# Second batch of a fused attention and MoE kernel: softmax sums by products with ones, maxima joined by selection products, values ordered anew

## The chip, the cores and the metric

The kernel runs on one core of a Trainium2 chip. Its time is the device time of one launch in microseconds (us), as the median of several runs; lower is better. PE is the engine for matrix products, PEld its weight loads, DVE the vector engine, ACT the scalar engine with its table functions, POOL the general engine GpSimd, SP the engine that starts most DMA transfers. Products write to PSUM, everything else on the chip stands in SBUF.

## The reference

Eight batches of eight heads, 512 local and 32 global positions, head size 64. Local queries see the global keys and a window of 32 keys to each side; global queries see all keys. Both are softmaxed with a maximum subtracted and 1e-9 added to the sum. The result goes through a dense layer, a softplus and a second dense layer.

```python
s_g = scale * matmul(q_g, k_all.T);  out_g = matmul(sm(s_g), v_all)
s_ll = where(abs(pos[:, None] - pos[None, :]) <= 32, scale * matmul(q_l, k_l.T), -1e9)
s_l = concatenate([scale * matmul(q_l, k_g.T), s_ll], axis=-1)
out_l = matmul(sm(s_l), concatenate([v_g, v_l]))
x = concatenate([out_g, out_l], axis=2).transpose(0, 2, 1, 3).reshape(B * S, H * D)
h = x @ w_in;  g = maximum(h, 0) + log1p(exp(-abs(h)));  return g @ w_out
```

Here x has 4352 rows of 512, w_in is 512 x 2048 and w_out 2048 x 512. All inputs are float32; the two weights arrive as float64.

## The kernel before

**Dense layers.** The local rows of a batch (512 tokens) are one block, the 256 global rows of all batches one more at the end. For batch b and slice f of 16, a tile `h` of 128 x 512 is summed by twelve products (x and w each split into a high and a low part), in two halves of six; `act` makes the softplus from it (ACT `e`, DVE `e` L533, ACT `gh`, POOL `gl`), and four `opart` calls of three products add g times w_out to four tiles o0 to o3. The tiles `h` take turns in two PSUM slots (tag "h"); o0 to o3 have a bank each.

**Weights.** The float64 words are taken apart while batch 0 runs: per tile of 128 x 512 one ACT operation (L470), one one-input DVE operation (L477), two two-input ones (L479, L482), an ACT cast (L487) and a POOL subtract (L488). Their names are wbitswi, wiraw, wbitswo, woraw with the slice's number.

**Attention.** A pair m of heads is worked on at once; m = 0 to 3 are batch 0, which has code of its own (`turn0`, `split0`, and for the global queries `evict0g` with its tiles p0g1gh and p0g1gl, and `values0g` with o0g). Pairs from 4 on go through five pieces. `scores` (two halves p) writes keys by queries into a two-bank PSUM tile, to which for m < `MPE` = 8 the mask is added by a product; ACT copies it to s (L310), and DVE takes the maxima of 32 x 32 squares, turned (mt, L313). `maxima` has POOL copy three quadrants of mt to the first (L325), DVE reduces what belongs to a window (L328 to L332) and copies the result to all four quadrants (L338). `probs` spreads it by transposes (mb, L346), POOL subtracts (L355, L357) and ACT takes the exp (L358). `sums` does the same as `maxima` with sums of squares of the exps (zt, L368), adds 1e-9 (L371), inverts (L375) and spreads (rb, L377). `values` writes 32 PE instructions of values into v_ps, and DVE multiplies by rb into xa (L396). Scores, v_ps and the turned probabilities of batch 0 share one PSUM tile of two banks (tag "a"), so each waits until the one before was read.

**Order.** PE's order is that of the program. The dense items of batch 0 are written one after another, and between them the attention pieces whose due number is reached: pair m has its scores at 12m and 12m + 6 (with maxima and probs), its sums at 12m + 14, its values at 12m + 21. Every product has one line of the profile, L132, so PE's rows are told apart by tile names. The order of the other engines is made by a scheduler from the program.

Of the kernel before, what the change touches and what calls it, by code (L numbers as in the profile page):

```python
# [63 lines left out]
def moe_over_global_local_attention(  # L64
# [258 lines left out]
    def gather(mt, op):  # L323
        for a in range(1, 4):
            nc.gpsimd.tensor_copy(mt[0:32, GW * a:GW * a + GW], mt[32 * a:32 * a + 32, 0:GW])  # L325
        e0 = 4 * GW + 1
        for u, off in ((-1, 2), (2, 3)):
            nc.vector.tensor_reduce(grid(mt, e0 + u, (7, 6), (1, 2)), grid(mt, 4 + u - 2 * (u < 0), (12, 6), (1, 2), (off, 2), (GW, 4)), axis=AX.XY, op=op)  # L328
# [34 lines left out]

    def sums(m):
# [12 lines left out]
        nc.vector.transpose(rb.rearrange("p (s k) -> p s k", k=32), zr[:, 0:19].unsqueeze(2).to_broadcast([P, 19, 32]))  # L377
# [24 lines left out]
    def end(m):  # L402
        return 12 * m + 8 + LAG_V

    def pieces():
# [6 lines left out]
        for m in range(M0, M):  # L412
            for p in range(NPC):
# [3 lines left out]
                if p == 1:  # L417
                    fs.append(lambda m=m: maxima(m))
                    fs += [lambda m=m, q=q: probs(m, q) for q in range(NPC)]
                ps.append((12 * m + 6 * p, piece(*fs)))  # L420
            ps.append((12 * m + 8 + LAG_Z, lambda m=m: sums(m)))
# [323 lines left out]
```

## Time and profile before

| | us |
|---|---|
| median of 3 runs | 990.09 (990.07 to 990.39) |
| profiled execution | 991.48 |
| its span on the core | 989.7 |
| PE busy in it | 946.2 |
| DVE busy | 643.1 |
| ACT busy | 492.6 |
| POOL busy | 469.5 |

The profile is of one execution, and the runs' median is 1.39 below it. A row of a timeline has the start, the length, the engine, the line, the operation, the tiles (result, then inputs), the count, and in brackets the idle time before it with what ended it. Matmul rows of a group overlap, since the products are pipelined: how long a group occupies PE is the distance from its start to the next start. The table of slices on the page:

```profile
PE   6998598889999999999999999999999999999998
```

Each digit is a slice of 24.7 us, in tenths busy. Batch 0's own attention ends in the fourth slice, and pairs 4 to 7 stand in slices three to nine.

### The profile page before, as it was taken

To read this page: it belongs to the slowest core of one execution; us is meant where nothing else is said; L and a number is where in the kernel's file an instruction comes from. 1 tells how busy PE (TensorE), PEld (TensorE's weight loads), DVE (VectorE), ACT (ScalarE), POOL (GpSimd) and SP (SyncE) were. 2 spreads that over 40 slices of the span, in tenths; PEclk is the share of its full clock that TensorE was granted. 3 is DMA by queue.
4 is the path that set the end of the run, shared out by engine and by line. 5 is a ranking of instruction groups with operands and counts; after the bars stand their busy time and mean duration, and the time that the engine had idled before them with its cause. 6 is when DMAs were issued, how large, how long until landed. Compare 5 with 4: busy or idle time off the path is not lost.

```text
span 989.7 us, 14732 instructions
## 1 busy us (share of the span) xinstructions
PE 946.2 (96%) x5476; PEld 763.8 (77%) x5476; DVE 643.1 (65%) x1193; ACT 492.6 (50%) x811; POOL 469.5 (47%) x648
## 2 busy tenths in 40 slices
PE   6998598889999999999999999999999999999998
PEld 4776476668888788878887888878887888888896
DVE  5869898896667756786669666776668665411211
ACT  5756466544444544454445444454454445444453
POOL 4437776655445544444445544554445444322221
PEclk8998899999999999999999999999999999999999
DMA  9651331211112211121112111121112100100000
GB/s 357 231 188 46 122 111 57 65 66 41 47 47 69 69 47 46 48 74 47 47 37 72 47 47 47 66 71 47 47 33 88 32 17 1 65 1 1 10 35 22
DMA packets 30697, 64.60 MB, mean 65 GB/s; under 512 B 7328, under 2 KB 7840, under 8 KB 30624
## 3 DMA queue, kind: packets, MB, share of 16 engines
q1 hardware_dynamic: 29888, 63.32, 19.0%
q8 instruction: 43, 0.70, 0.3%
q10 hardware_dynamic: 736, 0.33, 0.2%
q14 instruction: 30, 0.25, 0.1%
HBM read 54.20 MB, written 9.44 MB: 64 GB/s over the span
## 4 chain that ended last, share of the span: by engine, by line
PE 67%; DVE 9%; POOL 4%; issue 3%; ACT 1%; DMA 1%; POOLq 0%; DVEq 0%; ACTq 0%
PE o L132 30%; PE h L132 29%; PE s_ps L132 5%; PE v_ps L132 4%; DVE xh L442 1%; DVE zt L368 1%; DVE xl L443 1%; POOL xl L443 1%; DVE mb L346 1%; POOL mt L325 1%; DVE s L312 1%; POOL s L355 1%; DVE xa L396 1%; DVE mt L332 0%; DVE e L533 0%
## 5 line engine op out<-in xcount | busy, mean ns | idle before, releaser
L132 PE MATMUL h<-xh,wi 128*128 128x512 f32 (+1 forms) x1152 | 341.9, 380 | 6.5 <-DVE e L533 5.8
L132 PE MATMUL o<-wo,gh 128*128 128x512 f32 x1088 | 344.8, 398 | 0.0
L537 POOL TENSOR_TENSOR gl<-e,gh 128x512 fp32r<-128x512 f32 x136 | 180.5, 1327 | 315.7 <-ACT gh L536 263.2
L132 PEld LDWEIGHTS h<-xh,wi 128*128 128x128 f32 x1152 | 211.1, 188 | 51.8 <-DVE e L533 8.9
L132 PEld LDWEIGHTS o<-wo,gh 128*128 128x128 f32 x1088 | 198.8, 188 | 46.0 <-issue 3.3
L533 DVE SCALAR_TENSOR_TENSOR e<-h,e 128x512 f32<-128x512 f32 x136 | 92.7, 682 | 210.1 <-ACT e L532 192.5
L132 PE MATMUL h<-xl,wi 128*128 128x512 f32 (+1 forms) x576 | 217.6, 378 | 0.9 <-DVE xl L443 0.9
L132 PE MATMUL o<-wo,gl 128*128 128x512 f32 x544 | 213.1, 392 | 0.2
L530 ACT ACTIVATE e<-h 128x512 f32<-128x512 f32 x136 | 81.0, 595 | 175.5 <-PE h L132 173.5
L536 ACT CAST gh<-e 128x512 fp32r<-128x512 f32 x136 | 84.5, 622 | 154.7 <-DVE e L533 154.5
L132 PEld LDWEIGHTS h<-xl,wi 128*128 128x128 f32 x576 | 108.4, 188 | 21.7 <-DVE xl L443 1.3
L355 POOL TENSOR_TENSOR s<-s,mb 128x640 f32<-128x640 f32 (+1 forms) x56 | 96.6, 1725 | 57.8 <-DVE mb L346 57.8
L132 PEld LDWEIGHTS o<-wo,gl 128*128 128x128 f32 x544 | 102.4, 188 | 23.2 <-POOL gl L537 1.1
L368 DVE TRANSPOSE_TENSOR_REDUCE zt<-s 128x32 f32<-128x1024 f32 x56 | 69.4, 1239 | 58.9 <-ACT s L358 58.7
L358 ACT ACTIVATE s<-s 128x1024 f32<-128x1024 f32 x56 | 59.4, 1061 | 83.5 <-POOL s L357 47.7
L532 ACT ACTIVATE e<-e,one 128x512 f32<-128x512 f32 x136 | 98.4, 723 | 4.3
L531 ACT ACTIVATE e<-e 128x512 f32<-128x512 f32 x136 | 85.9, 632 | 3.9
L313 DVE TRANSPOSE_TENSOR_REDUCE mt<-s 128x32 f32<-128x1024 f32 x56 | 68.9, 1231 | 3.7 <-ACT s L310 2.9
L132 PE MATMUL s_ps<-raw 64*128 64x192 f32 (+2 forms) x672 | 64.3, 325 | 0.6 <-issue 0.6
L132 PEld LDWEIGHTS v_ps<-s,v 128*64 128x64 f32 x896 | 49.4, 137 | 19.5 <-ACT s L310 6.5
L132 PE MATMUL v_ps<-s,v 128*64 128x96 f32 (+3 forms) x896 | 56.7, 280 | 7.3 <-ACT s L310 5.2
L132 PEld LDWEIGHTS s_ps<-raw 64*128 64x128 f32 x672 | 53.5, 192 | 11.6 <-issue 10.8
(147 smaller groups left out, 886.0 us busy)
## 6 DMA issues: line engine op xcount, KB each, us to landing
raw<-in_qk SPq DMA_DIRECT2D x32, 352.0 KB, 3.0
v<-in_v SPq DMA_DIRECT2D x28, 384.0 KB, 3.0
raw<-in_qk SPq DMA_DIRECT2D x28, 368.0 KB, 3.6
wiraw<-in_w_in SPq DMA_DIRECT2D x16, 512.0 KB, 8.5
woraw<-in_w_out SPq DMA_DIRECT2D x16, 512.0 KB, 7.4
out<-ot SPq DMA_DIRECT2D x32, 256.0 KB, 2.1
v<-in_v SPq DMA_DIRECT2D x4, 512.0 KB, 8.6
raw<-in_qk SPq DMA_DIRECT2D x4, 416.0 KB, 8.3
```

What stands on the lines that cost most here:

```text
L132: order["pe"] = after(nc.tensor.matmul(*a, **k), "pe").ins
L313: order["scores"] = nc.vector.tensor_reduce(windows(mt, 4 + 16 * p, 36, 2, 16), s.rearrange("p h (b k) -> p h b k", k=32), axis=AX.X, op=A ...
L355: nc.gpsimd.tensor_tensor(sw, sw, pairs(mb, 352, mo, md, w), op=ALU.subtract)
L358: nc.scalar.activation(s, s, AF.Exp, scale=0.125)
L368: nc.vector.tensor_reduce(windows(zt, 4 + 16 * p, 36, 2, 16), st["s", m, p].rearrange("p h (b k) -> p h b k", k=32), axis=AX.X, op=ALU.add ...
L443: (nc.vector if j % 2 else nc.gpsimd).tensor_tensor(lo, f(t), hi.bitcast(F32), op=ALU.subtract)
L530: nc.scalar.activation(e, ph, AF.Abs)
L531: nc.scalar.activation(e, e, AF.Exp, scale=-1.0)
L532: nc.scalar.activation(e, e, AF.Ln, bias=one)
L533: nc.vector.scalar_tensor_tensor(e, ph, 0.0, e, op0=ALU.max, op1=ALU.add)
L536: nc.scalar.copy(gh, e)
L537: nc.gpsimd.tensor_tensor(gl, e, gh.bitcast(F32), op=ALU.subtract)
```

## The change

For pairs 4 to 7 alone, three things are done in another way.

*Sums.* Instead of `sums`, `values` makes the sums itself: 16 products of the exps with a block of ones go to z_ps, a tile in an "h" slot, and to the free half of v_ps's second bank. There each sum stands on 64 rows. DVE then transposes 32 x 32 squares of both out of PSUM (z), adds 1e-9, joins the three parts of a global query's sum, inverts all 19 columns at once (zr) and spreads them (rb) as before.

*Maxima.* Four products with 0/1 matrices (`quads`) copy each quadrant of mt to all 128 rows of a PSUM tile m_ps (tag "a"). DVE's reductions read that and leave the result on all rows, so the POOL copies L325 and the DVE copies L338 are not needed. `quads` is filled by a POOL copy at the start.

*Order.* Maxima and probs of a pair are due at 12m + 8 (before: with the second scores at 12m + 6), values at 12m + 15 (before 12m + 21), where before them sums stood at 12m + 14. The tiles mb have three buffers instead of two. The start of batch 1's pieces (`first`) keeps its value. On SP's queue the v loads and the xg stores of these pairs come to stand ahead of some raw and weight loads.

```diff
+LAG_M = 2
+EARLY_V = 15
...
+    quads = const.tile([P, 4, P], F32, name="quads")
+    ones = const.tile([P, D], F32, name="ones")
+    nc.vector.memset(ones, 1.0)
+    one = ones[:, 0:1]
...
+        nc.gpsimd.tensor_copy(quads.rearrange("p a (c k) -> p a c k", c=4),
+                              identf.rearrange("p (a k) -> p a k", a=4).unsqueeze(2).to_broadcast([P, 4, 4, 32]))
...
-    def gather(mt, op):
-        for a in range(1, 4):
-            nc.gpsimd.tensor_copy(mt[0:32, GW * a:GW * a + GW], mt[32 * a:32 * a + 32, 0:GW])
+    def gather(mt, op, src=None):
+        rows = P if src is not None else 32
+        if src is None:
+            src = mt
+            for a in range(1, 4):
+                nc.gpsimd.tensor_copy(mt[0:32, GW * a:GW * a + GW], mt[32 * a:32 * a + 32, 0:GW])
         e0 = 4 * GW + 1
+        to = lambda start, *dims: grid(mt, start, *dims, rows=rows)
+        of = lambda start, *dims: grid(src, start, *dims, (GW, 4), rows=rows)
...
     def maxima(m):
-        e = gather(st.pop(("mt", m)), ALU.max)
+        mt = st.pop(("mt", m))
+        if m < MPE:
+            ps = ps_a.tile([P, 2, 512], F32, tag="a", name=f"m_ps{m}")[:, 0]
+            for a in range(4):
+                mm(ps[:, GW * a:GW * a + GW], lhsT=quads[:, a], rhs=mt[:, 0:GW], start=True, stop=True, skip_group_check=True)
+            st["e", m] = gather(mt, ALU.max, ps)
+            return
+        e = gather(mt, ALU.max)
...
-        mb = pl.tile([P, 2, 352], F32, tag="mb", name=f"mb{m}_{p}", bufs=2)
+        mb = pl.tile([P, 2, 352], F32, tag="mb", name=f"mb{m}_{p}", bufs=3)
...
+    def weighted(m, banks, lhs, seen):
+        for c, p, o, w, bank, at in VPARTS:
+            for h in range(2):
+                mm(banks[bank][64 * h:64 * h + 64, at:at + w], lhsT=lhs(h, c), rhs=st["s", m, p][:, h, o:o + w],
+                   start=(bank, h) not in seen, stop=(c, bank) in ((3, 0), (5, 1)), skip_group_check=True)
+                seen.add((bank, h))
+
+    def sums_pe(m, zs):
+        z = pl.tile([P, rows_of(608)], F32, tag="mb", name=f"z{m}", bufs=3)[:, 0:608]
+        for t, at, w in ((zs[0], 0, 384), (zs[1], 384, 224)):
+            nc.vector.transpose(z[:, at:at + w], t[:, 0:w])
+        zr = pl.tile([P, ROW], F32, tag="zr", name=f"zr{m}", bufs=2)
+        nc.vector.tensor_scalar(zr[:, 0:19].unsqueeze(2), windows(z, 0, 32, 19, 1), 1e-9, None, op0=ALU.add)
+        nc.vector.tensor_reduce(zr[:, 19:20], windows(z, 128, 224, 3, 1).rearrange("p a b -> p b a"), axis=AX.X, op=ALU.add)
+        nc.vector.tensor_scalar(windows(zr, 4, 7, 3, 1), zr[:, 19:20].unsqueeze(1).to_broadcast([P, 3, 1]), 1e-9, None, op0=ALU.add)
+        nc.vector.reciprocal(zr[:, 0:19], zr[:, 0:19])
+        spread(m, zr)
...
         ps = ps_a.tile([P, 2, 512], F32, tag="a", name=f"v_ps{m}")
-        parts = ((0, 0, 0, 160, 0, 0), (1, 0, 160, 192, 0, 64), (2, 0, 352, 160, 0, 192), (2, 1, 0, 32, 0, 352), (3, 1, 32, 96, 0, 288),
-                 (3, 1, 128, 96, 1, 0), (4, 1, 224, 192, 1, 32), (5, 1, 416, 96, 1, 128))
-        seen = set()
-        for c, p, o, w, bank, at in parts:
-            for h in range(2):
-                mm(ps[64 * h:64 * h + 64, bank, at:at + w], lhsT=vt[:, h, c], rhs=st["s", m, p][:, h, o:o + w],
-                   start=(bank, h) not in seen, stop=(c, bank) in ((3, 0), (5, 1)), skip_group_check=True)
-                seen.add((bank, h))
+        if m < MPE:
+            zs = (ps_h.tile([P, 512], F32, tag="h", name=f"z_ps{m}"), ps[:, 1, 256:512])
+            weighted(m, zs, lambda h, c: ones, set())
+        weighted(m, (ps[:, 0], ps[:, 1]), lambda h, c: vt[:, h, c], {(1, 0), (1, 1)} if m < MPE else set())
+        if m < MPE:
+            sums_pe(m, zs)
...
-        return 12 * m + 8 + LAG_V
+        return 12 * m + (EARLY_V if m < MPE else 8 + LAG_V)
...
+                tail = [lambda m=m: maxima(m)] + [lambda m=m, q=q: probs(m, q) for q in range(NPC)] if p else []
+                if m < MPE:
+                    if p:
+                        ps.append((12 * m + 6 + LAG_M, piece(*tail)))
+                    tail = []
+                ps.append((12 * m + 6 * p, piece(*fs, *tail)))
+            if m >= MPE:
+                ps.append((12 * m + 8 + LAG_Z, lambda m=m: sums(m)))
...
-    first = end(H // 2 - 1) + STEP
+    first = 12 * (H // 2 - 1) + 8 + LAG_V + STEP
```

Three places of the new order follow; the new file's lines are some 8 to 48 higher (L132 is L140).

PE around pair 4's values, before: h0_5 is the tile of slice 5, v_ps4 the values, o0_0 the first output tile.

```order
L132 MATMUL h0_5_1087<-xh0_3_627,wi5_613 128x512 x2
L132 MATMUL h0_5_1087<-xl0_3_628,wi5_613 128x512
L132 MATMUL v_ps4_1129<-s4_0_655,v4_145 64x160 x2
L132 MATMUL v_ps4_1129<-s4_0_655,v4_145 64x192 x2
L132 MATMUL v_ps4_1129<-s4_0_655,v4_145 64x160 x2
L132 MATMUL v_ps4_1129<-s4_1_703,v4_145 64x32 x2
L132 MATMUL v_ps4_1129<-s4_1_703,v4_145 64x96 x4
L132 MATMUL v_ps4_1129<-s4_1_703,v4_145 64x192 x2
L132 MATMUL v_ps4_1129<-s4_1_703,v4_145 64x96 x2
L132 MATMUL o0_0_889<-wo3_774,gh0_3_949 128x512 x2
```

After, the ones_73 products into z_ps4 and v_ps4 come first, then the values, and all of it stands in the middle of the output products of slice 1 (gh0_1, gl0_1).

```order
L140 MATMUL o0_1_894<-wo1_517,gl0_1_806 128x512
L140 MATMUL z_ps4_971<-s4_0_657,ones_73 64x160 x2
L140 MATMUL z_ps4_971<-s4_0_657,ones_73 64x192 x2
L140 MATMUL z_ps4_971<-s4_0_657,ones_73 64x160 x2
L140 MATMUL z_ps4_971<-s4_1_705,ones_73 64x32 x2
L140 MATMUL z_ps4_971<-s4_1_705,ones_73 64x96 x2
L140 MATMUL v_ps4_970<-s4_1_705,ones_73 64x96 x2
L140 MATMUL v_ps4_970<-s4_1_705,ones_73 64x192 x2
L140 MATMUL v_ps4_970<-s4_1_705,ones_73 64x96 x2
L140 MATMUL v_ps4_970<-s4_0_657,v4_146 64x160 x2
L140 MATMUL v_ps4_970<-s4_0_657,v4_146 64x192 x2
L140 MATMUL v_ps4_970<-s4_0_657,v4_146 64x160 x2
```

The group has moved ahead from between h0_5 and the outputs of slice 3 to between the first and last two outputs of slice 1.

DVE in the stretch in which mb4 (pair 4's spread maxima) is made and p0g1gl, the small copy for the last global output of batch 0, follows; before:

```order
L346 STREAM_TRANSPOSE mb4_1_724<-mt4_653 128x2x320
L479 SCALAR_TENSOR_TENSOR wbitswi8_877<-wiraw8_683,wbitswi8_877 128x512
L482 SCALAR_TENSOR_TENSOR wiraw8_683<-wiraw8_683,wbitswi8_877 128x512
L533 SCALAR_TENSOR_TENSOR e0_1_799<-h0_1_760,e0_1_799 128x512
L368 TENSOR_REDUCE zt4_963<-s4_0_655 128x2x16
L477 TENSOR_SCALAR wbitswo3_769<-wbitswo3_769 128x512
L255 COPY p0g1gl_815<-t0g1_808 32x128
L479 SCALAR_TENSOR_TENSOR wbitswo3_769<-woraw3_153,wbitswo3_769 128x512
```

After, from behind the second mb4:

```order
L524 SCALAR_TENSOR_TENSOR wbitswi8_878<-wiraw8_685,wbitswi8_878 128x512
L522 TENSOR_SCALAR wbitswo4_821<-wbitswo4_821 128x512
L527 SCALAR_TENSOR_TENSOR wiraw8_685<-wiraw8_685,wbitswi8_878 128x512
L524 SCALAR_TENSOR_TENSOR wbitswo4_821<-woraw4_681,wbitswo4_821 128x512
L575 SCALAR_TENSOR_TENSOR e0_1_800<-h0_1_740,e0_1_800 128x512
L522 TENSOR_SCALAR wbitswi10_1062<-wbitswi10_1062 128x512
L527 SCALAR_TENSOR_TENSOR woraw4_681<-woraw4_681,wbitswo4_821 128x512
L524 SCALAR_TENSOR_TENSOR wbitswi10_1062<-wiraw10_876,wbitswi10_1062 128x512
L522 TENSOR_SCALAR wbitswo5_838<-wbitswo5_838 128x512
L527 SCALAR_TENSOR_TENSOR wiraw10_876<-wiraw10_876,wbitswi10_1062 128x512
L524 SCALAR_TENSOR_TENSOR wbitswo5_838<-woraw5_683,wbitswo5_838 128x512
L263 COPY p0g1gl_816<-t0g1_809 32x128
```

The first sums of pair 4 (zt4) are gone; p0g1gl now stands behind ten weight operations and e0_1, where there were three, e0_1 and the reduction for zt4.

DVE where xa of pair 4 (xa1_0) is made, before: rb4 stood long ahead, and xa stands behind the maxima's transposes of pair 5.

```order
L346 STREAM_TRANSPOSE mb5_0_1064<-mt5_906 128x704
L346 STREAM_TRANSPOSE mb5_1_1069<-mt5_906 128x2x320
L479 SCALAR_TENSOR_TENSOR wbitswo8_1121<-woraw8_953,wbitswo8_1121 128x512
L533 SCALAR_TENSOR_TENSOR e0_5_1110<-h0_5_1087,e0_5_1110 128x512
L396 TENSOR_TENSOR xa1_0_1146<-v_ps4_1129,rb4_981 128x384
L396 TENSOR_TENSOR xa1_0_1146<-v_ps4_1129,rb4_981 128x224
L479 SCALAR_TENSOR_TENSOR wbitswo9_1175<-woraw9_1002,wbitswo9_1175 128x512
```

After, where z4 is the tile of the turned sums and zr4 its inverse:

```order
L415 STREAM_TRANSPOSE z4_1004<-v_ps4_970 128x224
L527 SCALAR_TENSOR_TENSOR wiraw11_929<-wiraw11_929,wbitswi11_1107 128x512
L417 TENSOR_SCALAR zr4_1007<-z4_1004 128x19
L418 TENSOR_REDUCE zr4_1007<-z4_1004 128x1
L419 TENSOR_SCALAR zr4_1007<-zr4_1007 128x3
L420 RECIPROCAL zr4_1007<-zr4_1007 128x19
L386 STREAM_TRANSPOSE rb4_1012<-zr4_1007 128x608
L438 TENSOR_TENSOR xa1_0_1014<-v_ps4_970,rb4_1012 128x384
L438 TENSOR_TENSOR xa1_0_1014<-v_ps4_970,rb4_1012 128x224
L575 SCALAR_TENSOR_TENSOR e0_4_1051<-h0_4_1028,e0_4_1051 128x512
```

xa now follows its own sums directly, ahead of e0_4, and the maxima of pair 5 come later.

More of the change, by code (lines that the diff above doesn't have):

```diff
@@ L315, in scores, with grid @@
         st["s", m, p] = s
-    def grid(t, start, *dims):
-        base = t[0:32, start:start + 1]
+    def grid(t, start, *dims, rows=32):
+        base = t[0:rows, start:start + 1]
         return bass.AP(base.tensor, base.offset, [list(base.ap[0])] + [list(d) for d in dims])
-    def gather(mt, op):
-        for a in range(1, 4):
-            nc.gpsimd.tensor_copy(mt[0:32, GW * a:GW * a + GW], mt[32 * a:32 * a + 32, 0:GW])
+    def gather(mt, op, src=None):
[4 more added lines that the diff above has]
+                nc.gpsimd.tensor_copy(mt[0:32, GW * a:GW * a + GW], mt[32 * a:32 * a + 32, 0:GW])
@@ L330, in gather @@
+        nc.vector.tensor_reduce(to(e0 + 1, (7, 6), (4, 2)), of(4 + 1, (12, 6), (7, 2)), axis=AX.X, op=op)
         g = e0 + 42
-        nc.vector.tensor_reduce(grid(mt, g, (1, 2)), grid(mt, 4 + 4, (36, 2), (12, 3), (3, 2), (GW, 4)), axis=AX.XYZ, op=op)
-        nc.vector.tensor_copy(grid(mt, e0 + 4, (21, 2), (7, 3)), mt[0:32, g:g + 2].unsqueeze(2).to_broadcast([32, 2, 3]))
+        nc.vector.tensor_reduce(to(g, (1, 2)), of(4 + 4, (36, 2), (12, 3), (3, 2)), axis=AX.XYZ, op=op)
+        order["maxima"] = nc.vector.tensor_copy(to(e0 + 4, (21, 2), (7, 3)), mt[0:rows, g:g + 2].unsqueeze(2).to_broadcast([rows, 2, 3])).ins
@@ L362, in moe_over_global_local_attention, with spread @@
     SEG = ((lambda t: t[:, 0:128].unsqueeze(1), 0, 1, 128), (lambda t: windows(t, 160, 224, 2, 192), 128, 2, 192))
+    def spread(m, zr):
+        rb = st["rb", m] = pl.tile([P, rows_of(608)], F32, tag="rb", name=f"rb{m}", bufs=1)[:, 0:608]
+        nc.vector.transpose(rb.rearrange("p (s k) -> p s k", k=32), zr[:, 0:19].unsqueeze(2).to_broadcast([P, 19, 32]))
     def sums(m):
@@ L375, in sums @@
             nc.vector.reciprocal(zr[32 * a:32 * a + 32, 0:19], z[0:32, 21 * h:21 * h + 19])
-        rb = st["rb", m] = pl.tile([P, rows_of(608)], F32, tag="rb", name=f"rb{m}", bufs=1)[:, 0:608]
-        nc.vector.transpose(rb.rearrange("p (s k) -> p s k", k=32), zr[:, 0:19].unsqueeze(2).to_broadcast([P, 19, 32]))
+        spread(m, zr)
+    VPARTS = ((0, 0, 0, 160, 0, 0), (1, 0, 160, 192, 0, 64), (2, 0, 352, 160, 0, 192), (2, 1, 0, 32, 0, 352), (3, 1, 32, 96, 0, 288),
+              (3, 1, 128, 96, 1, 0), (4, 1, 224, 192, 1, 32), (5, 1, 416, 96, 1, 128))
+    def weighted(m, banks, lhs, seen):
[13 more added lines that the diff above has]
+        nc.vector.reciprocal(zr[:, 0:19], zr[:, 0:19])
+        spread(m, zr)
     def values(m):
@@ L416, in pieces @@
                     fs.append(lambda m=m, p=p: load(m + 1, p))
[L417 to L421, printed above, removed]
+                tail = [lambda m=m: maxima(m)] + [lambda m=m, q=q: probs(m, q) for q in range(NPC)] if p else []
[6 more added lines that the diff above has]
+                ps.append((12 * m + 8 + LAG_Z, lambda m=m: sums(m)))
             fs = [lambda m=m: values(m)]
@@ L479, in bits_w @@
         note("dve", nc.vector.scalar_tensor_tensor(a, hi32, -0x80000000, a, op0=ALU.bitwise_and, op1=ALU.bitwise_or))
-        r = lo32 if k < NF - 1 else pl.tile([P, 512], I32, tag="mb", name=f"wlast{kind}", bufs=2)
+        r = lo32 if k < NF - 1 else pl.tile([P, 512], I32, tag="mb", name=f"wlast{kind}", bufs=3)
         note("dve", nc.vector.scalar_tensor_tensor(r, lo32, 29, a, op0=ALU.logical_shift_right, op1=ALU.bitwise_or))
@@ L497, in output_banks @@
         return banks["o"]
-    one = const.tile([P, 1], F32, name="one")
-    nc.vector.memset(one, 1.0)
     def moe_items():
```

5 lines of the change are left out of this document (2 added, 3 removed).

## The prediction

> **What bounds the kernel now.** I read the page first, its busy times and shares of the span of 989.7 us.
>
> ```profile
> PE 946.2 (96%) x5476; PEld 763.8 (77%) x5476; DVE 643.1 (65%) x1193; ACT 492.6 (50%) x811; POOL 469.5 (47%) x648
> ```
>
> TensorE (PE) is busy for 96% of the span, so whatever is added to PE costs its own length unless PE would have been idle there. The second view is the list of PE's waits, by what ended them (total us, times, longest).
>
> ```profile
> PE s_ps L132 <- DVE xa L396: 8.8, 2, 7.5
> PE h L132 <- DVE e L533: 5.8, 8, 1.7
> PE v_ps L132 <- ACT s L310: 5.2, 3, 3.4
> ...
> PE o0g L132 <- ACT p0g1gh L254: 2.7, 1, 2.7
> PE v_ps L132 <- DVE s L312: 2.1, 1, 2.1
> ...
> PE h L132 <- DVE xl L443: 0.9, 1, 0.9
> ```
>
> The third is a table of windows (length; busy time of PE, PEld, DVE, ACT, POOL with counts; granted PE clock; DMA share; GB/s).
>
> ```profile
> 120.37:124.11 3.74, 3.74 (x17) 2.49 (x18) 3.74 (x4) 1.57 (x3) 3.74 (x6) 0.54 0.00 0
> 77.41:83.52 6.11, 6.11 (x26) 4.83 (x26) 6.11 (x10) 5.65 (x11) 3.25 (x6) 0.66 0.13 50
> 217.00:989.00 772.00, 765.20 (x4350) 623.69 (x4348) 459.92 (x863) 368.80 (x565) 342.50 (x491) 1.00 0.14 45
> ```
>
> From 217 us on PE is busy for 765.20 of 772 us at a clock of 1.00, and the instructions there stay as they are: that stretch keeps its length. What the change can move lies before 217 us, and DVE is busy throughout both windows quoted from there. The timeline of PE around the stalls (start, length, what, count, idle time before and its releaser):
>
> ```profile
> 102.09 0.73 PE L132 MATMUL h<-xh,wi 128*128 128x512 f32 x2 [1.19 <-DVE e L533]
> ...
> 106.50 2.03 PE L132 MATMUL v_ps<-s,v 128*64 128x160 f32 x32 [1.40 <-ACT s L310]
> 108.46 0.73 PE L132 MATMUL o<-wo,gh 128*128 128x512 f32 x2
> ...
> 120.37 1.03 PE L132 MATMUL s_ps<-mask,ident 128*128 128x512 bf16 x2 [7.54 <-DVE xa L396]
> ```
>
> **What PE gains in work.** Four pairs (m = 4 to 7) each get 16 more products of the same shapes as the values products, with a block of ones in the place of v. A values group takes 108.46 - 106.50 = 1.96 us, so 4 x 1.96 = 7.8. Each also gets four selection products, 128 x 128 against 76 columns, two instructions apiece. The trace has none of that shape; the nearest is the turning of the probabilities, 128 columns:
>
> ```profile
> 70.32 1.39 PE L132 MATMUL t0g<-diag,e_g 128*128 128x128 f32 x10
> 71.64 0.74 PE L132 MATMUL h<-xh,wi 128*128 128x512 f32 x2
> ...
> 231.01 2.72 PE h L132 x12
> 233.74 1.36 PE o L132 x6
> ```
>
> Ten of them occupy 71.64 - 70.32 = 1.32, or 0.132 each; 4 x 8 x 0.132 = 4.2. The ends: no better than half that (76 of 128 columns are 0.6 of it, say 1.9 in all), no worse than a 512-column product (2.72 / 12 = 0.227, so 7.3). I take 4.2, the nearest row. Together **+12.0** (9.7 to 15.1).
>
> **What goes.** The waits on xa, on s (ACT and DVE), and on xl are 8.8 + 5.2 + 2.1 + 0.9 = 17.0, and the one of 1.19 at 102.09 lies in the same stretch: 18.2. They belong to places where values, xa and the scores behind them are ordered anew: values come earlier, sums no longer hang on POOL copies and two reductions of 1.2 us, so the old waits don't survive as such (which new ones appear is the next part). After the 7.54 wait PE ran at 0.54 of its clock for 3.74 us, which lost 3.74 x 0.46 = 1.7. A first pair of products after a wait shows 0.73, where others show 0.62: ten such places, 1.1. Together **-21.0**.
>
> A rule of the Trainium skill speaks to that clock: "TensorE: Matmul & The Clock Gate", in its section on HAM oscillation, has an idle window of about 3.4 us send the clock to half rate. The trace agrees for the wait of 7.54 (0.54 after it), but a wait of only 2.72 ahead of 77.41 also left 0.66, which the rule would not give. By the rule 1.7 would return and nothing else; the sum above takes the same 1.7.
>
> **What is new.** First the last global output, o0g1. Its second half needs p0g1gl, a small DVE copy.
>
> ```profile
> 72.29 1.55 DVE L479 SCALAR_TENSOR_TENSOR wbitswi<-wiraw,wbitswi 128x512 int32<-128x512 int32 x1
> 73.88 1.39 DVE L482 SCALAR_TENSOR_TENSOR wiraw<-wiraw,wbitswi 128x512 int32<-128x512 int32 x1
> 75.19 0.68 DVE L533 SCALAR_TENSOR_TENSOR e<-h,e 128x512 f32<-128x512 f32 x1
> ...
> 77.44 0.27 DVE L255 COPY p0g1gl<-t0g 32x128 f32<-32x128 f32 x1
> ...
> 80.46 0.68 DVE L479 SCALAR_TENSOR_TENSOR wbitswi<-wiraw,wbitswi 128x512 int32<-128x512 int32 x1
> ```
>
> Before, mb ends at 72.29 and the copy starts at 77.44. In the new order of DVE the copy stands behind seven two-input weight operations, three one-input ones and one e. The groups of this stretch give their means (busy us, mean ns):
>
> ```profile
> L482 DVE SCALAR_TENSOR_TENSOR woraw<-woraw,wbitswo 128x512 int32<-128x512 int32 x13 | 12.9, 1001 | 0.1
> ...
> L477 DVE TENSOR_SCALAR wbitswo<-wbitswo 128x512 int32<-128x512 int32 x13 | 9.4, 739 | 0.2 <-ACT wbitswo L470 0.2
> ...
> L377 DVE STREAM_TRANSPOSE rb<-zr 128x608 f32<-128x608 f32 x3 | 2.4, 800 | 0.0
> ```
>
> That is 7 x 1.00 + 3 x 0.74 + 0.68 = 9.9. mb itself ends 0.9 later than before: the selection products wait for half of h1 (1.36) and take 1.06, while copies of 1.56 (L338) go. So the copy ends at 72.29 + 0.9 + 9.9 + 0.27 = 83.4. The old gl products started 1.04 after 77.41, at 78.45; PE has 1.06 of selection products more ahead of them, which this wait swallows. New wait: 83.4 - 78.45 - 1.06 = **3.9** (0 if the operations take 0.68 and 0.43 each, 8 if each takes the 1.55 of the row at 72.29).
>
> Second, the chain from the sums to xa, at the place where the next scores want the same PSUM slot. For pair 4: two transposes out of PSUM (0.8 together, as the one of 608 columns), two weight triples that stand between (2 x (1.00 + 1.00 + 0.74) = 5.5 at the means, 2 x (0.68 + 0.68 + 0.43) = 3.6 unhindered), four small operations (0.9), the spread of the reciprocals (0.80) and two products to xa (0.9): 8.9, or 7.0 unhindered. PE covers it with the last six of the products with ones (0.7), v (1.96), o (1.36) and h (2.72): 6.7. That leaves 0.3 to 2.2 ahead of s5_1 and as much ahead of s6_1, which has the same cover; pairs 6 and 7 have another o or h and fewer weights between, so nothing. I take 0.6 for the first (PE is late there already by the wait above, while DVE works on) and 1.2 for the second: **1.8** (0 to 6, if operations double).
>
> Third, the products with ones need pair 5's exponentials, which now have from m5 to z5: four h halves and four o pairs of 1.36 each, and the scores of pair 6, two mask products at 0.227 and twelve of about 176 columns, 0.227 x 176 / 512 = 0.08 each: 10.9 + 1.4 = 12.3 us of PE work. The old kernel's row for pair 5 has its reductions at 113.17 and its last exp ending at 126.43:
>
> ```profile
> 113.17 0.53 DVE L328 TENSOR_REDUCE mt<-mt 32x12 f32<-32x96 f32 x2 [3.05 <-POOL mt L325]
> ...
> 125.37 1.06 ACT L358 ACTIVATE s<-s 128x1024 f32<-128x1024 f32 x1
> ```
>
> 13.26 against 12.3: **0.9** (0 to 3, as the queues fall). The new mask of quads on POOL pushes an early select back: 0.2. The DVE reductions that go (two of 1.2 us per pair), the three quadrant copies and POOL's gather copies free DVE time, but PE waits for DVE only where named, so they enter by the waits and not a second time. SP's order moves the xg stores and v loads of these pairs ahead of some raw and weight loads; in the windows above DMA is 0.13 or less busy, so nothing. New: 3.9 + 1.8 + 0.9 + 0.2 = **+6.8**.
>
> **The sum.** 12.0 + 6.8 - 21.0 = -2.2. The profiled execution took 991.48 us, 1.39 above the median of 990.09; it would take 989.3, and on the median's scale the forecast is 990.1 - 2.2 = **987.9**.
>
> **Rivals.** *The new waits don't come.* DVE has some 4 us less to do per pair and unhindered operations take 0.68; then the 6.8 fall away: 990.1 + 12.0 - 21.0 = 981.1. For it: 80.46 shows the short time right there, where POOL had nothing to do. Against it: DVE is busy all of both early windows. *DVE's two-input operations are held by POOL (slower).* The same operation took 1.55 at 72.29 and 0.68 at 80.46; at 72.29 POOL was in this:
>
> ```profile
> 71.72 1.58 POOL L355 TENSOR_TENSOR s<-s,mb 128x640 f32<-128x640 f32 x1 [1.78 <-DVE mb L346]
> ```
>
> The new order places the seven beside the same POOL subtracts, in one queue ahead of p0g1gl. If all 7 and the 8 of the two chains are held to 1.55 instead of their mean of 1.00, that is 15 x 0.55 = 8.3 more: -2.2 + 8.3 = +6.1, so 996.2. POOL was busy for 3.25 + 3.74 of the 9.85 us of the two early windows, 0.71: held for that share, their mean is 0.71 x 1.55 + 0.29 x 0.68 = 1.30, which adds 15 x 0.30 = 4.5 and gives 992.4. I price this rival midway, at 994.3. It turns the sign once their mean passes 1.00 + 2.2 / 15 = 1.15 us. The Trainium skill has this as a rule ("SBUF — State Buffer", section "Who interferes with whom"): a DVE operation with two SBUF inputs and GpSimd shut each other out for the whole instruction. The two rows agree; by it the slower rival is the outcome wherever POOL is busy. *The waits only change their names*: the products with ones wait for the exps and PE's added 12.0 fill what was idle, one for one; about 990. *The change doesn't act*: the new code covers only m < 8 and the rows of the order show it there; no chance of note.
>
> **How the numbers follow.** Forecast 0.44, first rival 0.22, slower rival 0.24, change of names 0.10. A measurement of this kernel can tell 0.2%, 2.0 us, from no change, so faster means under 988.1. The forecast lies at that edge: its 0.44 are 0.24 faster and 0.20 the same. Faster: 0.24 + 0.22 = 0.46. The same: 0.20 + 0.07 = 0.27. Slower: 0.24 + 0.03 = 0.27. The range of 8 in 10 takes in the first rival's time and the slower one's with a little of the selection products' upper end: 981.0 to 994.8. Above it lies the part of the slower rival in which everything is held, below it only a gain past the first rival. The bounds of the unknown shapes (9.7 to 15.1) alone give 985.6 to 991.0, inside it.
>
> **What would show it.** Right: a group of products with ones takes 1.96 and one of selection about 1.06; p0g1gl ends near 83 and o0g waits for it; the wait of 7.54 is gone; waits on xa of about 1 us ahead of s5_1 and s6_1; DVE's busy time falls by some 15 us; the stretch after the last pair of the second batch is as long as before. Wrong: any single new wait over 5 us, a clock under 0.9 in a window past 90 us, weight operations of DVE at a mean of 1.15 or more (slower rival) or 0.8 or less (first rival), or selection products at 0.23 each.

## The result and the profile after

The changed kernel took **1008.07 us** (median; 1005.39 to 1008.85) against 990.08 before: a ratio of 1.0177, 95% interval 1.0157 to 1.0196. The prediction was 987.9, its range 981.0 to 994.8; it was wrong by 20 us and in the sign.

The page of the profile after, and PE's waits (total us, times, longest):

```profile
span 1006.6 us, 14966 instructions
...
PE 961.3 (95%) x5629; PEld 779.7 (77%) x5636; DVE 632.1 (63%) x1157; ACT 493.4 (49%) x811; POOL 459.7 (46%) x621
```

```profile
PE z_ps L140 <- DVE e L575: 11.0, 2, 7.4
PE o0g L140 <- ACT p0g1gh L262: 5.7, 1, 5.7
...
PE h L140 <- DVE e L575: 4.0, 6, 1.1
PE s_ps L140 <- DVE xa L438: 3.3, 2, 3.0
...
PE o0g L140 <- DVE p0g1gl L263: 2.2, 1, 2.2
```

The waits of the old list on xa (8.8), s (7.3) and xl (0.9) are gone or small, as the prediction had it. But PE's idle time, span less busy, was 989.7 - 946.2 = 43.5 before and is 1006.6 - 961.3 = 45.3 now: other waits of the same sum stand in their place. The span grew by 16.9, of which idle time is 1.8 and PE's busy time 15.1. How much of the latter is new work shows in PE's timeline:

```profile
83.17 1.97 PE L140 MATMUL o0g<-p0g1gh,v 128*128 128x64 f32 x8 [5.66 <-ACT p0g1gh L262]
...
87.36 0.68 PE L140 MATMUL o0g<-p0g1gl,v 32*128 32x64 f32 x2 [2.23 <-DVE p0g1gl L263]
...
101.64 1.37 PE L140 MATMUL z_ps<-s,ones 128*64 128x160 f32 x20
102.84 0.82 PE L140 MATMUL v_ps<-s,ones 128*64 128x96 f32 x12
103.50 1.98 PE L140 MATMUL v_ps<-s,v 128*64 128x160 f32 x32
...
120.37 1.01 PE L140 MATMUL m_ps<-mt,quads 128*128 128x76 f32 x8
121.17 0.71 PE L140 MATMUL h<-xh,wi 128*128 128x512 f32 x2
...
141.52 2.51 PE L140 MATMUL z_ps<-s,ones 128*64 128x160 f32 x20 [7.43 <-DVE e L575]
```

At full clock the products with ones occupy 103.50 - 101.64 = 1.86 and the selection products 121.17 - 120.37 = 0.80: 4 x 2.66 = 10.6 for four pairs. The other 15.1 - 10.6 = 4.5 are put down to slow clock, by subtraction. The windows show where (length; busy PE, PEld, DVE, ACT, POOL; granted PE clock; DMA share; GB/s), after first, before second:

```profile
80.00:100.00 20.00, 14.25 (x57) 11.48 (x59) 13.10 (x18) 11.43 (x20) 11.53 (x10) 0.66 0.09 29
100.00:125.00 25.00, 21.66 (x150) 17.68 (x150) 15.46 (x29) 11.59 (x18) 7.43 (x7) 0.93 0.37 131
125.00:150.00 25.00, 17.42 (x119) 13.94 (x119) 22.25 (x23) 11.14 (x17) 17.34 (x14) 0.80 0.17 57
...
235.00:1006.00 771.00, 764.07 (x4345) 622.74 (x4343) 458.60 (x861) 367.07 (x563) 340.83 (x491) 1.00 0.14 45
```

```profile
80.00:100.00 20.00, 20.00 (x93) 15.10 (x93) 19.93 (x33) 11.15 (x20) 12.94 (x11) 0.84 0.11 32
100.00:125.00 25.00, 14.88 (x86) 10.88 (x86) 21.75 (x31) 12.32 (x20) 17.86 (x18) 0.86 0.29 107
```

Two things are to be seen. The last row of after is as long and as dense as the old one from 217 on, so all of the loss lies ahead of it. And DVE, which was busy for 41.7 of the 45 us from 80 to 125, is now busy for 28.6 there, and then for 22.25 of 25 from 125 to 150, where PE stands for 7.43 in one piece: its load has become uneven. That bunch, ahead of z5 at 141.52, in DVE's timeline:

```profile
122.18 1.09 DVE L522 TENSOR_SCALAR wbitswo<-wbitswo 128x512 int32<-128x512 int32 x3
123.18 1.63 DVE L366 STREAM_TRANSPOSE mb<-mt 128x704 f32<-128x704 f32 x2
124.74 2.98 DVE L524 SCALAR_TENSOR_TENSOR wbitswo<-woraw,wbitswo 128x512 int32<-128x512 int32 x2
127.64 2.05 DVE L522 TENSOR_SCALAR wbitswi<-wbitswi 128x512 int32<-128x512 int32 x1
...
137.65 1.52 DVE L524 SCALAR_TENSOR_TENSOR wbitswi<-wiraw,wbitswi 128x512 int32<-128x512 int32 x1
139.20 1.66 DVE L527 SCALAR_TENSOR_TENSOR wiraw<-wiraw,wbitswi 128x512 int32<-128x512 int32 x1
140.79 0.68 DVE L575 SCALAR_TENSOR_TENSOR e<-h,e 128x512 f32<-128x512 f32 x1
```

Five weight triples stand between pair 5's maxima and e0_6, the operation that frees the "h" slot for z_ps5. The exponentials are not what z5 waits for: ACT's last one ended at 134.19, when PE had just stopped. ACT is itself late by the same bunch. Its last two steps ahead of e0_6 (the later one at 138.23) stand in its order behind a weight's cast, and ahead of that cast it was idle for 1.93, until DVE had made the weight:

```profile
133.12 1.07 ACT L378 ACTIVATE s<-s 128x1024 f32<-128x1024 f32 x1
134.08 0.59 ACT L572 ACTIVATE e<-h 128x512 f32<-128x512 f32 x1
136.60 0.65 ACT L532 CAST wi<-wiraw 128x512 fp32r<-128x512 f32 x1 [1.93 <-DVE wiraw L527]
...
138.23 0.72 ACT L574 ACTIVATE e<-e,ones 128x512 f32<-128x512 f32 x1
```

### The profile page after: what moved, and what is told of

The parts are those of the page before. It is cut to its first block, busy times and chain, and to the rows that moved or that the text cites. A ratio compares the mean times of both kernels' runs of the same rounds, so it can differ in the third digit from the quotient of the medians.

```text
span 1006.6 us, 14966 instructions
## 1 busy us (share of the span) xinstructions
PE 961.3 (95%) x5629; PEld 779.7 (77%) x5636; DVE 632.1 (63%) x1157; ACT 493.4 (49%) x811; POOL 459.7 (46%) x621
## 4 chain that ended last, share of the span: by engine, by line
PE 75%; DVE 15%; issue 4%; ACT 3%; POOL 2%; DMA 1%; ACTq 0%; POOLq 0%; DVEq 0%
PE o L140 32%; PE h L140 31%; PE s_ps L140 6%; PE v_ps L140 4%; DVE xh L487 1%; ACT e L180 1%; DVE mb L366 1%; DVE xl L488 1%; DVE zt L392 1%; DVE wbitswo L524 1%; DVE e L575 1%; DVE sums L177 1%; DMA wiraw<-in_w_in 1%; DVE wbitswi L524 1%; DVE woraw L527 1%
## 5 line engine op out<-in xcount | busy, mean ns | idle before, releaser
L140 PE MATMUL h<-xh,wi 128*128 128x512 f32 (+1 forms) x1152 | 342.4, 381 | 5.6 <-DVE e L575 4.0
L140 PE MATMUL o<-wo,gh 128*128 128x512 f32 x1088 | 344.9, 398 | 0.0
L579 POOL TENSOR_TENSOR gl<-e,gh 128x512 fp32r<-128x512 f32 x136 | 177.4, 1304 | 331.7 <-ACT gh L578 281.9
L140 PEld LDWEIGHTS h<-xh,wi 128*128 128x128 f32 x1152 | 211.1, 189 | 50.1 <-DVE e L575 6.5
L140 PEld LDWEIGHTS o<-wo,gh 128*128 128x128 f32 x1088 | 198.7, 188 | 46.1 <-issue 3.4
L140 PE MATMUL h<-xl,wi 128*128 128x512 f32 (+1 forms) x576 | 217.9, 378 | 0.0
L140 PE MATMUL o<-wo,gl 128*128 128x512 f32 x544 | 212.8, 391 | 0.0
L140 PEld LDWEIGHTS h<-xl,wi 128*128 128x128 f32 x576 | 108.5, 188 | 20.5
L140 PEld LDWEIGHTS o<-wo,gl 128*128 128x128 f32 x544 | 102.4, 188 | 22.3 <-POOL gl L579 0.2
L574 ACT ACTIVATE e<-e,ones 128x512 f32<-128x512 f32 x136 | 98.3, 723 | 4.3
L392 DVE TRANSPOSE_TENSOR_REDUCE zt<-s 128x32 f32<-128x1024 f32 x48 | 59.6, 1241 | 55.2 <-ACT s L378 55.2
L140 PE MATMUL s_ps<-raw 64*128 64x192 f32 (+2 forms) x672 | 64.2, 324 | 0.6 <-issue 0.4
L320 DVE TENSOR_TENSOR s<-s_ps,mask 128x1024 f32<-128x1024 f32 x48 | 58.2, 1213 | 6.6 <-PE s_ps L140 6.6
L140 PEld LDWEIGHTS s_ps<-raw 64*128 64x128 f32 x672 | 53.5, 192 | 10.6 <-issue 10.6
L377 POOL TENSOR_TENSOR s<-s,mb 128x384 f32<-128x384 f32 (+2 forms) x84 | 58.7, 712 | 0.0
```

The source lines that it names most:

```text
L140: order["pe"] = after(nc.tensor.matmul(*a, **k), "pe").ins
L377: nc.gpsimd.tensor_tensor(s[:, :, so:so + w], s[:, :, so:so + w], mb[:, :, mo:mo + w], op=ALU.subtract)
L392: nc.vector.tensor_reduce(windows(zt, 4 + 16 * p, 36, 2, 16), st["s", m, p].rearrange("p h (b k) -> p h b k", k=32), axis=AX.X, op=ALU.add ...
L574: nc.scalar.activation(e, e, AF.Ln, bias=one)
L579: nc.gpsimd.tensor_tensor(gl, e, gh.bitcast(F32), op=ALU.subtract)
```

## The experiments

All are edits of the changed kernel; the ratios are to the kernel before, with 95% intervals. `zs` are the tiles of the sums, "pin" is the rule by which a weight tile's first DVE operation stands behind the last maxima that the program has written.

### Is it the "h" slot, the chain on DVE, or the loads?

**e4_noslot** takes z_ps out of the "h" slots.

```diff
...
-            zs = (ps_h.tile([P, 512], F32, tag="h", name=f"z_ps{m}"), ps[:, 1, 256:512])
+            zs = (ps[:, 1, 256:512], ps[:, 1, 256:512])
...
```

> The changed kernel, but the products with ones all go to the free half of the second bank of v_ps, over one another (sums and so outputs are not the reference's); the tile z_ps in an h slot is gone, its transposes read 192, 192 and 224 columns instead of 384 and 224. Theory A (the h slot: z_ps waits until the softplus of the tile before has left it): the waits of z_ps on DVE e, 11.0 us, go and with them some 3 us of half clock after 141.5 and 174.5; about 994 us against 1008. Theory B (the exponentials are late and the slot is only the name of the wait): PE stands at the same place until the exps are done, the wait reads ACT s L378 and stays 5 us or more; 1004 or more. Theory C (the products' own length and the stall ahead of o0g1 make nearly all of it): 1003 to 1006.

Measured: 1011.24 us, 1.0200 (1.0181 to 1.0219). The waits of z_ps are gone, and PE meets the same bunch one step later:

```profile
134.79 2.03 PE L140 MATMUL v_ps<-s,ones 128*64 128x160 f32 x32
...
151.80 0.61 PE L140 MATMUL s_ps<-mask,ident 128*128 128x512 bf16 x1 [8.83 <-DVE xa L442]
```

The slot is only where the wait shows. Theory A fell; so did B, for nothing waited for the exps. The 1003 to 1006 of theory C was missed as well: the time is no shorter at all.

**e7_nochain** leaves out all DVE work between the products with ones and xa.

```diff
-            sums_pe(m, zs)
+            st["rb", m] = ones[:, 0:1].to_broadcast([P, 608])
```

> The changed kernel with all its products, but nothing reads the sums: the two transposes out of PSUM, the small operations, the inversion and the spread are left out for pairs 4 to 7, and xa is the values times one (outputs are not the reference's). Theory A (the DVE chain between the products with ones and xa, which now stands between the values and the release of their PSUM slot, costs the time): about 990 to 995, the products' 11 to 12 us against the old stalls; waits of PE on xa under 3 us. Theory B (the products and the early place cost it): 1002 or more, as the changed kernel's 1008 less the chain's own 4 x 4 us of DVE time that PE never waited for.

Measured: 1006.04 us, 1.0161 (1.0145 to 1.0177). That was the theory I held at this point, and it fell: with four chains gone, the time is 2 us shorter, and the two intervals overlap. PE comes to z5 sooner and waits longer:

```profile
115.53 1.01 PE L140 MATMUL m_ps<-mt,quads 128*128 128x76 f32 x8
...
140.31 2.50 PE L140 MATMUL z_ps<-s,ones 128*64 128x160 f32 x20 [11.05 <-DVE e L575]
```

Meanwhile DVE, in its own timeline, did little from 98 to 116 (it was busy for 3.76 of these 18 us), though two of the `wo` weights that it shifts right behind m5 (at 117.35) had been ready for it since ACT made their magnitudes, the last at 85.72 (ACT's timeline, in the second fence):

```profile
105.37 0.85 DVE L438 TENSOR_TENSOR xa<-v_ps,ones 128x384 f32<-128x384 f32 x2 [2.32 <-PE v_ps L140]
111.82 0.69 DVE L575 SCALAR_TENSOR_TENSOR e<-h,e 128x512 f32<-128x512 f32 x1 [5.60 <-ACT e L574]
...
117.35 1.13 DVE L522 TENSOR_SCALAR wbitswo<-wbitswo 128x512 int32<-128x512 int32 x3
```

```profile
85.72 0.67 ACT L515 ACTIVATE wbitswo<-woraw 128x512 f32<-128x512 f32 x1
```

The pin holds these two behind m5's maxima, so DVE's free time cannot take them up.

**e15_actq** moves the last weights' loads out of SP's queue, where after the change they stand behind keys that wait for s5_1.

```diff
-        after(nc.sync.dma_start(out=dst, in_=src), "load")
+        if k >= (13 if kind == "wi" else 10):
+            nc.scalar.dma_start(out=dst, in_=src)
+        else:
+            after(nc.sync.dma_start(out=dst, in_=src), "load")
```

> The changed kernel; the loads of the last weights (w_in from slice 13, w_out from slice 10) are started from ACT's queue instead of SP's, where they stand behind the second scores' keys of pair 6 and so behind s5_1 and xa of pair 4 (they started at 114.8 there, 97.5 before the change). DVE's order stays as it is. Theory S (the late weights leave DVE idle and then make the burst that PE waits for): the burst thins out, z5 starts at most 3 us after h7's first half, time under 1002. Theory D (DVE's order is what counts: five weight triples stand between pair 5's maxima and z5, whether loaded or not): no change within 2 us, 1006 to 1010.

Measured: 1011.15 us, 1.0198 (1.0174 to 1.0221); z_ps waits 11.0 with a longest of 7.4, as before. The late loads are real (114.8 instead of 97.5), but moving them returned nothing: theory D's reading held, its 1006 to 1010 was missed by 1 us.

### DVE's order

**e13_nopin** drops the pin; **e16_actq_nopin** does so on top of e15.

```diff
-        note("dve", i) if tight else after(i, "maxima")
+        note("dve", i)
```

> The changed kernel without the rule that a weight tile's first DVE operation stands behind the last maxima written before it. The triples of wo8 and wo9 then stand ahead of p0g1gl (10 weight operations there become 14), and pair 5's burst has three triples instead of five. Theory D: the wait of z_ps 5 (7.4) falls to under 3 while the one ahead of o0g1 (7.9) grows by some 4: about the same, 1003 to 1009. Theory S: the burst is set by the loads and the wait of z_ps stays over 5; 1008 to 1013.

> Both edits together: the last weights loaded from ACT's queue, and their DVE operations free of the maxima. Between pair 5's maxima and z5 stand two triples (wi12, wi13) instead of five. Theory D: z_ps 5 waits under 2 us instead of 7.4, o0g1 some 4 us longer; about 1000. If neither the triples nor the loads count (theory P: PE's round trip to DVE and back is simply longer than the work that covers it), the wait of z_ps stays over 4 and the time over 1005.

Measured: e13 999.73 us, 1.0090 (1.0074 to 1.0106); e16 1000.53 us, 1.0090 (1.0072 to 1.0108). In e13 the two triples that the pin held back run earlier, and z5 hardly waits:

```profile
135.05 1.37 PE L140 MATMUL z_ps<-s,ones 128*64 128x160 f32 x20 [1.61 <-DVE e L575]
```

Eight of the 18 us come back by nothing but DVE's order. The 1003 to 1009 expected of e13 was missed, since the wait ahead of o0g1 didn't grow (5.1 + 0.7). The loads add nothing here either; e16 came out at the 1000 that theory D gave it.

**e8_pinned** holds the weights behind xa, so that none stands within the chain; **e20_copyfirst** holds them behind the copy p0g1gl; **e22_both_orders** does both.

```diff
-            nc.vector.tensor_tensor(y[:, at:at + w], ps[:, bank, 0:w], rb[:, at:at + w], op=ALU.mult)
+            i = nc.vector.tensor_tensor(y[:, at:at + w], ps[:, bank, 0:w], rb[:, at:at + w], op=ALU.mult).ins
+            if m < MPE:
+                order["maxima"] = i
...
+        if n:
+            order["maxima"] = order["dve"]
```

> The changed kernel, with the weights' DVE operations that are written behind a pair's values held in DVE's order until behind its xa: no weight operation stands between the first transpose of z and xa any more (for pair 4 five of them did). If the weight operations inside the chain cost the time: waits of z_ps and of s_ps on xa fall from 14.3 to under 6 us, about 998 to 1001. If the time is lost because the chain starts late and DVE and PE wait for each other in turn, it stays at 1004 to 1010.

> The changed kernel, with the weight operations that are written behind the small copy p0g1gl held behind it in DVE's order: between mb4 and p0g1gl stands e0_1 alone instead of ten weight operations and e0_1. Theory D: o0g1's waits fall from 7.9 to under 3, and with them some 3 us of slow clock: 999 to 1002. If what is moved only comes back as a longer burst ahead of z5: 1005 or more.

> The edit of e20 and that of e8 (weights written behind a pair's values held behind its xa) together; products and places as in the changed kernel. Theory D: the two gains add, 4.4 of e8 and some 6 to 8 of e20: 995 to 998. What is left over 990 is then the products' 10.6 us less the old stalls that are filled.

Measured: e8 1003.64 us, 1.0132 (1.0116 to 1.0148); e20 1004.57 us, 1.0147 (1.0133 to 1.0161); e22 994.81 us, 1.0050 (1.0035 to 1.0065). Alone, each gives less than hoped: in e8 the waits of z_ps stay 9.3; in e20 the 7.9 ahead of o0g1 fall to 1.5, but waits on xa rise from 3.3 to 8.8. Both together return 13 us, more than their sum (4.4 + 3.5). PE's timeline in e20 shows why: the weight operations that no longer stand ahead of the copy stand within pair 4's chain, and the next scores wait for its xa for 6.51, where the changed kernel had 2.98:

```profile
107.21 0.61 PE L140 MATMUL s_ps<-mask,ident 128*128 128x512 bf16 x1 [6.51 <-DVE xa L440]
```

The edit of e8 removes just that stop: in e22 it is 0.52. PE's waits in e22:

```profile
PE z_ps L140 <- DVE e L579: 8.6, 2, 6.3
...
PE o0g L140 <- ACT p0g1gh L262: 1.4, 1, 1.4
```

Its PE is busy for 957.3 of a span of 992.6, so idle for 35.3, and 957.3 - 946.2 - 10.6 leaves 0.5 for slow clock. So with these two orders the 10.6 of products fill 43.5 - 35.3 = 8.2 us of old idle time, and the change still costs 4 to 5 us by the medians. The bunch ahead of z5 is not dissolved in e22: the wait there is still 6.3. No run joins its edits with that of e13.

### The parts alone

**e1_maxima**: old sums and values, selection products. **e2_sums**: old maxima, products with ones at the old place. **e3_late**: the whole change with values at the old place. **e5_order**: old maxima and sums at the new places. **e9_maxearly**: the change without products with ones.

```diff
-EARLY_V = 15
+EARLY_V = 21
...
-        if m < MPE:
-            zs = (ps_h.tile([P, 512], F32, tag="h", name=f"z_ps{m}"), ps[:, 1, 256:512])
-            weighted(m, zs, lambda h, c: ones, set())
-        weighted(m, (ps[:, 0], ps[:, 1]), lambda h, c: vt[:, h, c], {(1, 0), (1, 1)} if m < MPE else set())
-        if m < MPE:
-            sums_pe(m, zs)
+        weighted(m, (ps[:, 0], ps[:, 1]), lambda h, c: vt[:, h, c], set())
...
-        if m < MPE:
+        if False:
             ps = ps_a.tile([P, 2, 512], F32, tag="a", name=f"m_ps{m}")[:, 0]
```

The first piece alone is e3; the first two are e1; the first and third, with maxima at the old place (LAG_M = 0.01), e2; the last two e5; the second alone e9. With the second piece, `sums` is due for all pairs again. All five keep the third buffer of mb.

> Only the maxima by selection products, due 2 units later; sums and values as in the kernel before. Products cost 3.6 to 4.2. If the stall ahead of o0g1 (7.9 us against 2.7) comes from the maxima's later place, it shows here as well and the time is 996 to 999; if it comes from the weight operations that the missing sums let forward, it stays near 2.7 and the time is 989 to 993.

> Only the sums by products with ones, at the old place of the values (12m + 21), maxima by POOL copies as before. Products cost 7.5 to 7.8. If they fill PE's idle time, the old stalls of 7.54, 3.36 and 1.4 shrink and the time is 985 to 990; if the h slot stops PE here too, waits of z_ps on DVE e appear and the time is 996 or more.

> The changed kernel with the values back at 12m + 21 (EARLY_V 21): products with ones and selection products stay. If the early place of the values costs the time, the z_ps waits of 7.4 and 3.6 shrink to under 2 us in all and the time is about 996 (990 + 12 of products, less some waits), else, if the h slot is short at any place, it stays at 1004 to 1010.

> Only the order of the change: values at 12m + 15, maxima and probs at 12m + 8, but maxima with POOL copies and sums by DVE and POOL as in the kernel before (sums due at 12m + 14). No products are added. If the early place is what costs, PE waits for the reciprocals (v_ps on DVE or s_ps on xa 10 us or more): 998 or more. If the early place as such gains, as the removed wait of 7.5 on xa suggests: 982 to 988.

> The changed kernel without the products with ones: selection products and the early values stay, the sums are made by DVE and POOL as before. If the sums' products with their chain cost most: 990 to 995 (e5, the order alone, took 996.6 and selection products gain 1 to 3). If the early place does: 1000 or more.

| | us | ratio |
|---|---|---|
| e1_maxima | 988.72 | 0.9974 (0.9962 to 0.9985) |
| e5_order | 996.57 | 1.0060 (1.0042 to 1.0078) |
| e9_maxearly | 999.83 | 1.0095 (1.0082 to 1.0109) |
| e3_late | 1006.09 | 1.0153 (1.0126 to 1.0180) |
| e2_sums | 1008.89 | 1.0172 (1.0154 to 1.0190) |

In e1 the selection products, with the later place of the maxima, pay for themselves. The stall ahead of o0g1 is there all the same (5.2 + 1.1), so it needs no early sums or values; but the 996 to 999 that I tied to it didn't come. The new order costs 6 us without a single added product (e5), against my hope of a gain, and products with ones cost 17 us even at the old place. Prices depend on what else stands there: selection products on top of the new order cost 3 us (e5 to e9), and products with ones cost 8 on top of both (e9 to the changed kernel), but 17 on top of e1 (e3).

In e2 the z chain comes into pair 5's bunch: the products ended at 112.4, DVE's first transpose began at 124.78 and xa at 132.72, with PE idle for 8.67 ahead of the next scores. In e3 the waits on z_ps are gone, which was to be the sign that the early place costs the time. But the 996 that belonged to it didn't come: PE stops at the same bunch for 11.5, on xa. In e9 that place shows a wait of 10.8 on xa:

```profile
PE s_ps L140 <- DVE xa L433: 14.8, 2, 10.8
```

### A version that beats both

**e10_pair4** is e1 with POOL's copies for pair 4; **e18_best_nopin** is that without the pin, **e21_best_copyfirst** that with e20's edit.

```diff
-        if m < MPE:
+        if M0 < m < MPE:
             ps = ps_a.tile([P, 2, 512], F32, tag="a", name=f"m_ps{m}")[:, 0]
```

> Selection products for the maxima of pairs 5 to 7 alone; pair 4 has POOL copies (still due at 12m + 8); sums and values as before. The variant with all four pairs took 988.7 with 6.3 us of waits ahead of o0g1 and 6.6 of m_ps on DVE mt. If o0g1 is late because m_ps4 keeps DVE's reductions waiting for PE, its wait falls to about 3 and the time to 985 to 987; if because of the place of the maxima and the weight operations behind them, it stays at 988 to 990.

> Selection products for the maxima of pairs 5 to 7 only, sums and values as in the kernel before (the version that took 987.0), and weights free of the maxima. m_ps5 waited 5.0 there for DVE, o0g1 6.2. If the pin makes the bursts, the 5.0 falls to under 2 and the time to 983 to 985; if the scheduler only moves the burst ahead of o0g1, 987 to 990.

> Selection products for pairs 5 to 7 only, sums and values as in the kernel before (987.0), with the weight operations behind p0g1gl as in e20. Theory D: the 6.2 us of waits ahead of o0g1 fall to under 3 and 2 to 3 us of slow clock go with them: 982 to 985, faster than both kernels. Else 986 to 990.

Measured: e10 987.01 us, 0.9977 (0.9965 to 0.9989); e18 988.83 us, 0.9978 (0.9968 to 0.9989); e21 987.31 us, 0.9965 (0.9952 to 0.9977). In e10 o0g1 waits 6.2 all the same, so m_ps4 isn't what makes it late, and that the time reached the upper end of the 985 to 987 given for that case is luck (six of its ten runs lie at 987, four at 990). In e21 the wait is down to 1.8, but PE stops for others, and the 982 to 985 weren't reached:

```profile
PE m_ps L140 <- DVE mt L323: 8.5, 3, 4.7
PE h L140 <- DVE e L571: 6.7, 6, 3.9
...
PE o0g L140 <- ACT p0g1gh L262: 1.8, 1, 1.8
```

All three beat the kernel before by 0.2 to 0.35%, as e1 does by 0.26%; their intervals overlap, so which is best isn't settled, and neither order of DVE gained anything here that can be told from e10.

## Why the prediction was wrong

**The step that failed is "What is new", the +6.8.** The old waits went as "What goes" had it: those on xa, s and xl, 17.0, are off their places, and those on DVE's e ahead of h fell from 5.8 to 4.0, together 18.8 against 18.2. But the new waits are 11.0 of z_ps, 5.7 + 2.2 ahead of o0g1 where 2.7 was before, and 3.3 on xa: 19.5 instead of 6.8. Most of the gap is the third term, given as 0.9: it asked when pair 5's exponentials are ready, and they were ready (134.19, when PE stopped at 134.09). It left out that z_ps takes an "h" slot, which comes free only when DVE has done e0_6, behind five weight triples; that cost 7.43 at z5, and z6, to which nothing was given, 3.58.

The clock is the second term that failed. It was to give back 1.7 + 1.1; it took 4.5, since no new wait was given a price in clock. The 1.1 was misread besides: a first pair of 0.73 also stands where PE had not waited, behind a group of another shape (at 108.46 in the prediction's own rows; after the change 121.17 shows 0.71), so it isn't a price of the waits. The products, at 10.6 instead of 12.0, were nearly right. In all, PE's idle time was to fall by 18.2 - 6.8 = 11.4 and rose by 1.8: 13.2 of idle time and 7.3 of clock, less 1.4 of products, are the 19.1 between -2.2 and +16.9.

Why as much idle time came back: the largest of the new waits end, directly or by way of ACT, with a DVE operation that stands in DVE's order behind other work. DVE keeps to that order (in e7 it was idle for 5.60 while two weights were ready for it), and after the change the work comes in bunches, above all weight triples behind a pair's maxima. The old kernel's 7.54 was at the same place of the order, behind pair 5's maxima, though with less weight work in it: DVE first waited 3.05 for POOL's copies, and four weight operations stood ahead of xa, in DVE's timeline before:

```profile
114.81 1.10 DVE L477 TENSOR_SCALAR wbitswo<-wbitswo 128x512 int32<-128x512 int32 x3
...
117.38 1.57 DVE L479 SCALAR_TENSOR_TENSOR wbitswo<-woraw,wbitswo 128x512 int32<-128x512 int32 x1
...
119.48 0.84 DVE L396 TENSOR_TENSOR xa<-v_ps,rb 128x384 f32<-128x384 f32 x2
```

Taking away the slot (e4) or the early place (e3) moved the new stop on to xa, without the chain (e7) it grew, and the loads' delay (e15) made no difference to it; taking two triples out of the bunch (e13) cut it to 1.61. I read a wait's name as its cause.

**The slower rival** had the right sign, not the right mechanism. Two-input weight operations do get longer: in 60 to 200 us the four groups take 45.2 us for 41 operations, a mean of 1.10 against 45.0 for 46, 0.98, before. That is below the 1.15 that I set as its point, and 41 x 0.12 = 4.9 us of DVE time, when DVE was idle for far more. Of its own fifteen operations the seven ahead of p0g1gl took 8.45, a mean of 1.21, but the eight in the two chains 6.53, so the fifteen stand at 14.98, a mean of 1.00, which adds nothing to the sum. The longest it didn't name: the ten of the bunch ahead of z5, at 1.25. A row that held for it, and the copy:

```profile
77.13 2.29 DVE L527 SCALAR_TENSOR_TENSOR wiraw<-wiraw,wbitswi 128x512 int32<-128x512 int32 x1
...
87.04 0.27 DVE L263 COPY p0g1gl<-t0g 32x128 f32<-32x128 f32 x1
```

**"The waits only change their names"**, given 0.10, is nearest in mechanism; but its 990 let the products fill the idle time, which comes near only in e22 (8.2 of 10.6).

**The terms one by one.** o0g1: right in kind; the copy was to end at 83.4 and ended at 87.3, and PE's waits there are 5.66 + 2.23 = 7.9 against 2.7 + 3.9 forecast. The larger part is the wait for ACT's copy p0g1gh, which I had not timed. It ended at 83.1, because in ACT's order it stood behind the cast of a weight, for which ACT was idle until DVE's operation of 2.29 above was done; ACT's timeline:

```profile
79.46 0.66 ACT L532 CAST wi<-wiraw 128x512 fp32r<-128x512 f32 x1 [3.14 <-DVE wiraw L527]
```

xa: 3.3 against 1.8, with pair 4's four small operations at 2.85 instead of 0.9. z5 and z6: 11.0 against 0.9, as above. DVE's busy time fell by 11, not 15. SP's order "costs nothing" held for the loads, by e15. "A single new wait over 5 us" and "a clock under 0.9 past 90 us" were named as signs of a wrong forecast, and both came.

What stays open: that the order alone costs 6 us (e5) fits the bunches, but no profile shows its stops; whether the two orders of e22 would also help the kernel before was not run.

## What to carry to other kernels

A wait's releaser names the last link: before counting a wait as gone, look at how long the releasing engine has been busy without a gap ahead of it, and if it has, expect the same stop at the next place that needs that queue. Work added to an engine that waits fills its idle time only if what it waits for doesn't also lie behind that work; here four rounds of PE to DVE and back were added where sums used to be made off PE's path. (That the rounds by themselves cost the time is not shown: e7 left out DVE's part of them and gained 2 us.) When an engine's load falls and the time rises, look at its busy share window by window: the order in its queue can be worth more than the operations (8 and 13 us here, in e13 and e22, with not one operation changed).
